# SwiGLU feed-forward on one core: the first 256 tokens of x in two loads instead of one, and the order of the first weight loads

## The chip, the core and the metric

The kernel runs on one core of one Trainium2 chip. The metric is the device time of one execution in microseconds (us), lower is better. The kernel before was run three times: 119.38, 119.57 and 120.18 us, median 119.57. One more execution was profiled; the profile and the trace come from that one.

A core has five engines that run side by side and meet at semaphores: TensorE (PE in the profile; its weight loads are PEld), VectorE (DVE), ScalarE (ACT), GpSimd (POOL) and SyncE (SP). SyncE and ScalarE each issue loads and stores through a DMA queue of their own (SPq and ACTq in the profile).

## The reference

```python
B, S, D, F = 1, 2048, 512, 1376      # all inputs bf16

def reference(x, w_gate, w_up, w_down):
    g = silu(x @ w_gate)             # [S, F]
    u = x @ w_up                     # [S, F]
    return (g * u) @ w_down          # [S, D]
```

## The kernel before, in words

**Tiles.** The 2048 tokens are worked on in four chunks of 512 (`SC`). The 512 inputs (`D`) are four contraction steps of 128 (`dk`). The 1376 hidden columns (`F`) are ten full tiles of 128 (`ft`) and a rest of 96. For each chunk and tile TensorE computes a gate group (`G`) and an up group (`U`) transposed: the weights are stationary, x is moving, and the result has hidden columns on partitions and tokens along the row. Each group has one PSUM bank and consists, for each `dk`, of two matmuls, one for each half of 64 columns (`tile_position=(0, m)`), which run side by side in two column halves of the array (`gu_step`, L353). ScalarE takes the silu of the gate group, VectorE multiplies it by the up group into `hT_sb`. The rests of the four chunks are packed into X groups (L417) and Y groups (L428). When all chunks are through, TensorE runs the down projection from `hT_sb` and `wd_sb` (L464, in strips of 32 rows, and L441, L516), and VectorE and ScalarE copy the results to `o_sb`, from where they are stored. TensorE works its list of groups from front to back; the order is written out by hand.

**The head, where the change lies.** x must lie with its inputs on partitions (`xT_sb`). Chunks 1 to 3 come so by transposing loads. For chunk 0 a transposing load would be late, so its first 256 tokens (`HT`) are loaded as they are into `xn_sb`, and TensorE transposes them with an identity matrix (`ident`, from an iota by GpSimd and a comparison by VectorE).

- TensorE first runs `N_WARM` = 6 matmuls of 512 columns on constants (L367), then `N_FILL` = 2 pairs of 128 columns on two halves of 64 rows (L372).
- It waits for `xn` and for `ident`. Token 2p + j lies on partition p, place j, so that a partition gets one contiguous piece of 2 KB. For `dk` = 0, 1, 2 it transposes in halves of 64 rows, four per `dk` (L382, 12 in all, the two halves into two banks), for `dk` = 3 in halves of 64 columns (L390, 4 in all).
- VectorE copies the results of `dk` 0 and 2 from PSUM to `xT_sb`, ScalarE those of 1 and 3 (four copies of 128 x 256). The group list calls them T groups.
- The first four groups, `g0, u0, g1, u1` (tiles 0 and 1), run first over the 256 tokens that were transposed: both gates interleaved by `dk`, then both ups. Then they run over the other 256 tokens: `g0` in two pieces of 128 (waiting for `x0b`, then for `x0c`), the others in one of 256. From tile 2 on, each matmul has all 512 tokens.

**The queues.** ScalarE issues one load at the start, the first slab of gate weights (`wg0`, tiles 0 and 1, 256 KB). SyncE issues, in this order: `xn` (256 KB), `wu0` (256 KB), the transposing loads `x0b` and `x0c` (128 tokens each), and then the gate and up slabs of tiles 2 to 10, x of chunks 1 to 3, the down weights and the stores. A wait on a load (`need`) is put in front of the first matmul that uses it; all that stands behind it on TensorE waits too.

The stores of token tiles 0 and 1 go through `rows_of`, which undoes the 2p + j order: each writes every second row of the first 256.

Of the kernel before, what the change touches and what calls it, by code (L numbers as in the profile page):

```python
# [6 lines left out]
BF16 = mybir.dt.bfloat16  # L7
FP32 = mybir.dt.float32

N_WARM = 6  # L10
N_FILL = 2


def bass_standalone__swiglu_ffn__prompt_kernel(nc, x, w_gate, w_up, w_down, out):
    _, S, D = x.shape
    F = w_gate.shape[1]
    P = 128
    KD = D // P
# [3 lines left out]
    SC = 512  # L22
# [7 lines left out]
    HT = SC // 2  # L30
    HC = P // 2
    NXN = HT // P
    NB = 8
    NSG = 4
    NOS = 8
    assert D == 512 and S % SC == 0 and KD == 4 and F_LAST == 96 and NSC % 2 == 0

    xf = x[0]
    of = out[0]


    UPH = F + 32
# [4 lines left out]
    with ExitStack() as es:  # L47
# [4 lines left out]
        xT_sb = sb("xT_sb", [P, KD, S], BF16)  # L52
# [23 lines left out]
        s_P = sem("s_P")  # L76
# [4 lines left out]
        rest = list(range(4 * NOS))  # L81

        def take(i):
            rest.remove(i)
            return s_dma[i]

        s_out = [take(i) for i in (8, 1, 2, 3, 4, 5, 7, 6)]
        homes = dict(xn=14, x0b=22, wg0=30, x0c=13, wu0=21, wg2=29, wu2=20, wg4=12, wu4=28, wg6=19)
        loads = {}

        def load_sem(name):
            loads[name] = take(homes[name] if name in homes else rest[0])
            return loads[name]

        ones_w = nc.const_aps.tensor(1.0, [P, P], BF16)
        ones_m = nc.const_aps.tensor(1.0, [P, SC], BF16)
# [3 lines left out]
        def load_x(eng, name, t0, t1):  # L100
            eng.dma_start_transpose(
                xT_sb[:, :, t0:t1], xf[t0:t1, :]
            ).then_inc(load_sem(name), 16)

        def load_w(eng, name, src, base, f0, f1):
            eng.dma_start(
                w_sb[:, :, base + f0:base + f1],
                src[:, f0:f1].rearrange("(k p) f -> p k f", p=P),
            ).then_inc(load_sem(name), 16)

        slabs = [(0, 2), (2, 4), (4, 6), (6, 8), (8, NFT)]
        slab_of = {ft: a for a, b in slabs for ft in range(a, b)}

        def load_slab(eng, a, b):
            load_w(eng, f"wg{a}", w_gate, 0, a * P, min(b * P, F))
            load_w(eng, f"wu{a}", w_up, UPH, a * P, min(b * P, F - 32))

        def loads_on_scalar(act):
            load_w(act, "wg0", w_gate, 0, 0, slabs[0][1] * P)

        def loads_on_sync(sp):
            sp.dma_start(
                xn_sb[:, :, :].rearrange("p j d -> p (j d)"), xf[0:HT, :].rearrange("(p j) d -> p (j d)", j=NXN)
            ).then_inc(load_sem("xn"), 16)
            load_w(sp, "wu0", w_up, UPH, 0, slabs[0][1] * P)
            load_x(sp, "x0b", HT, HT + P)
            load_x(sp, "x0c", HT + P, SC)
            for a, b in slabs[1:]:
                load_slab(sp, a, b)
            load_w(sp, "wut", w_up, F - (F - 32), F - 32, F)  # L130
            for c in range(1, NSC):
                load_x(sp, f"x{c}", c * SC, (c + 1) * SC)
            sp.dma_start(
                wd_sb[:, 0:NFF, :], w_down[0:NFF * P, :].rearrange("(k p) d -> p k d", p=P)
            ).then_inc(load_sem("wd"), 16)
            for c in range(NSC):
# [7 lines left out]
        groups = []  # L144
# [1 line left out]
        act_ops, dve_ops = [], []  # L146

        def add_group(kind, **what):
            g = dict(kind=kind, at=len(groups), bank=banks[turn[(len(groups) - KD) % NB]], readers=[], **what)
            groups.append(g)  # L150
            return g

        def add_op(eng, g, **what):
            n_read[eng] += 1
            op = dict(g=g, at=n_read[eng], **what)
            (act_ops if eng == "A" else dve_ops).append(op)
            if g:
                g["readers"].append((eng, op["at"]))
            return op

        def tview(dk):
            return psum[:, 2 * dk:2 * dk + 2, 0:HC].bitcast(BF16).rearrange("p h (i t) -> p h i t", i=NXN)

        def tview_last():
            return psum[:, 6, 0:P].bitcast(BF16).rearrange("p (i t) -> p i t", i=NXN)

        sg_reader = []
        n_sg = 0
# [55 lines left out]
                t_ready[c] = d["at"]  # L224

        xt_ready = {}
        for dk in range(KD):
            g = add_group("T", dk=dk)
            eng = "DA"[dk % 2]
            out = xT_sb[:, dk, 0:HT]  # L230
            if dk < KD - 1:
                out, src = out.rearrange("p (i h t) -> p h i t", i=NXN, h=2), tview(dk)
            else:
                out, src = out.rearrange("p (i t) -> p i t", i=NXN), tview_last()
            op = add_op(eng, g, kind="copy", out=out, src=src, stored=(None, 0))
            xt_ready[dk] = (eng, op["at"])
        NT = len(groups)

        for c in range(NSC):
            for fts in [[0], [1], [2, 3]] + [[ft] for ft in range(4, NFF)]:  # L240
# [8 lines left out]
        for at in range(NST):  # L249
            j, c = divmod(at, NSC)  # L250
            t = c * TPC + j
            ob = at % NOS
            end = at == NST - 1
            for c0, c1 in [(0, LASTA), (LASTA, LASTB), (LASTB, D)] if end else [(0, D)]:
                g = add_group("O", t=t, c0=c0, c1=c1, c=c)
                (quads[j] if c0 == 0 else last).append(g)
                eng = "A" if (end and c0 == 0) or (j < TPC - 1 and c % 2) else "D"
# [6 lines left out]
            n_store[ob] += 2 if end else 1  # L264

        def rows_of(t):
            if t < NXN:
                return of[0:HT, :].rearrange("(p j) d -> j p d", j=NXN)[t]
            return of[t * P:(t + 1) * P, :]

        def on_sync(sp):
# [48 lines left out]
        def on_tensor(pe):  # L320
            landed = set()

            def need(name):
                if name not in landed:
                    pe.wait_ge(loads[name], 16)
                    landed.add(name)
# [13 lines left out]
            def gu_step(g, dk, n0, n1):  # L340
                c, ft = g["c"], g["ft"]
                if c > 0:
                    need(f"x{c}")
                if c == 0 and n1 > HT:
                    need("x0b")
                if c == 0 and n1 > HT + P:
                    need("x0c")
                need(("wg" if g["kind"] == "G" else "wu") + str(slab_of[ft]))
                if c == 0 and n0 < HT:
                    after(*xt_ready[dk])  # L350
                col = (0 if g["kind"] == "G" else UPH) + ft * P
                for m in (0, HC):
                    ins = pe.matmul(  # L353
                        g["bank"][m:m + HC, n0:n1], lhsT=w_sb[:, dk, col + m:col + m + HC],
                        rhs=xT_sb[:, dk, c * SC + n0:c * SC + n1], start=(dk == 0), stop=(dk == KD - 1),
                        tile_position=(0, m),
                    )
                if n1 == SC and dk == KD - 1:
                    ins.then_inc(s_P, 1)

            def gu_matmuls(g, n0, n1):
                for dk in range(KD):
                    gu_step(g, dk, n0, n1)
# [4 lines left out]

            warm(N_WARM, SC)
            for i in range(N_FILL):  # L370
                for h in range(2):
                    pe.matmul(  # L372
                        banks[NB - 2 + h][:, 0:P], lhsT=ones_w[h * HC:(h + 1) * HC, :],
                        rhs=ones_m[h * HC:(h + 1) * HC, 0:P], start=True, stop=True, tile_position=(h * HC, 0),
                    )
            need("xn")
            pe.wait_ge(s_J, 1)
            for dk in range(KD - 1):
                for i in range(NXN):
                    for h in range(2):  # L380
                        t0 = h * HC
                        ins = pe.transpose(  # L382
                            tview(dk)[:, h, i, :], xn_sb[t0:t0 + HC, i, dk * P:(dk + 1) * P],
                            ident[t0:t0 + HC, t0:t0 + HC],
                        )
                ins.then_inc(s_P, 1)
            for i in range(NXN):
                for m in (0, HC):
                    c0 = (KD - 1) * P + m
                    ins = pe.transpose(tview_last()[m:m + HC, i, :], xn_sb[:, i, c0:c0 + HC], ident[:, :])  # L390
            ins.then_inc(s_P, 1)

            g0, u0, g1, u1 = groups[NT:NT + 4]
            for dk in range(KD):
# [1 line left out]
                    gu_step(g, dk, 0, HT)  # L396
            for g in (u0, u1):
                gu_matmuls(g, 0, HT)
            gu_matmuls(g0, HT, HT + P)
            gu_matmuls(g0, HT + P, SC)  # L400
            for g in (u0, g1, u1):
                gu_matmuls(g, HT, SC)

            for g in groups[NT + 4:]:
# [149 lines left out]
```

## Time and profile before

| | before |
|---|---|
| runs | 119.38, 119.57, 120.18 us (median 119.57) |
| profiled execution | 120.14 us, span of the instructions 118.8 us |
| PE busy | 116.1 us (98%) |
| DVE, ACT busy | 43.4 us (37%), 35.5 us (30%) |
| first warm-up matmul, first transpose, first gate matmul | start at 0.77, 3.61, 4.40 us |
| DMA | 8.92 MB, mean 75 GB/s over the span |

Times in the trace count from the start of the span. The page gives each engine's busy time and the chain of work that ended last; the timeline gives starts and lengths; the DMA view gives what a transfer took from its issue to its landing, which is when the waiting engine may go on. A matmul's duration contains its way through the array and overlaps with the next one's, so rates are read from starts or counts, not from sums of durations. The granted clock in the profile is 1.00 for the whole span; half speed at the start shows only in the durations of matmuls.

### The profile page before, as it was taken

The page shows a single profiled execution, that of the slowest core. Times are in us where ns is not written, and L with a number is a line of the kernel's source. Part 1 is how long each engine was busy: PE and PEld are TensorE (multiplying, and loading weights), DVE is VectorE, ACT ScalarE, POOL GpSimd, SP SyncE. Part 2 cuts the span into 40 slices and gives each one's busy share as a digit, 9 for nine tenths or more (in the row PEclk, how much of TensorE's full clock was granted, in tenths as well). Part 3 has the DMA queues.
Part 4 walks back from the last instruction along what each step waited for, and adds up shares of the span by engine and source line. Part 5 has one row for each costly group of instructions (what it writes and reads, how often), then busy time and mean ns, then how long its engine had stood idle before and what let it go on. Part 6 is the DMA issues. An engine that isn't in the chain of part 4 may idle for free.

```text
span 118.8 us, 2992 instructions
## 1 busy us (share of the span) xinstructions
PE 116.1 (98%) x1343; PEld 65.9 (55%) x1344; DVE 43.4 (37%) x68; ACT 35.5 (30%) x61; POOL 0.4 (0%) x5
## 2 busy tenths in 40 slices
PE   7999999999999999999999999999999999999993
PEld 2795555555555555555555555554444444464452
DVE  0123533442524442534452444369800040214331
ACT  5234234264243274242355232470000030213001
POOL 1000000000000000000000000000000000000000
DMA  2999999992000000000000000000000022023612
GB/s 90 271 280 341 204 218 189 296 312 49 0 6 0 0 0 6 0 0 6 0 6 0 0 0 0 6 0 0 6 0 6 0 88 95 0 90 106 207 44 88
DMA packets 17596, 8.92 MB, mean 75 GB/s; under 512 B 8624, under 2 KB 17456, under 8 KB 17584
## 3 DMA queue, kind: packets, MB, share of 16 engines
q1 hardware_dynamic: 16912, 8.38, 27.9%
q10 hardware_dynamic: 672, 0.36, 1.0%
q8 instruction: 10, 0.16, 0.6%
q14 instruction: 2, 0.02, 0.0%
HBM read 4.81 MB, written 2.10 MB: 58 GB/s over the span
## 4 chain that ended last, share of the span: by engine, by line
PE 98%; issue 0%; DVE 0%
PE psum L353 59%; PE psum L464 24%; PE psum L441 7%; PE psum L417 3%; PE psum L367 2%; PE psum L428 1%; PE psum L390 0%; PE psum L372 0%; PE psum L382 0%; DVE o_sb L317 0%; PE psum L516 0%
## 5 line engine op out<-in xcount | busy, mean ns | idle before, releaser
L353 PE MATMUL psum<-xT_sb,w_sb 128*64 128x512 bf16 (+2 forms) x680 | 70.5, 369 | 0.0
L353 PEld LDWEIGHTS psum<-xT_sb,w_sb 128*64 128x64 bf16 x680 | 42.6, 111 | 27.1
L313 DVE TENSOR_TENSOR hT_sb<-sg_sb,psum 128x512 bf16<-128x512 f32 x40 | 27.5, 688 | 41.0 <-PE psum L353 36.6
L299 ACT ACTIVATE sg_sb<-psum 128x512 f32<-128x512 f32 x40 | 23.8, 596 | 41.2 <-PE psum L353 41.1
L464 PE MATMUL psum<-wd_sb,hT_sb 32*128 32x512 bf16 x480 | 26.9, 374 | 0.0
L464 PEld LDWEIGHTS psum<-wd_sb,hT_sb 32*128 32x128 bf16 x480 | 12.9, 93 | 13.1 <-issue 0.4
L317 DVE CAST o_sb<-psum 128x512 bf16<-128x512 f32 (+1 forms) x11 | 6.4, 603 | 25.2 <-PE psum L464 19.9
L299 ACT ACTIVATE o_sb<-psum 128x512 bf16<-128x512 f32 (+1 forms) x7 | 3.7, 580 | 32.9 <-PE psum L464 25.9
L441 PE MATMUL psum<-wd_sb,hT_sb 128*128 128x512 bf16 (+2 forms) x59 | 8.7, 307 | 0.2 <-issue 0.2
L441 PEld LDWEIGHTS psum<-wd_sb,hT_sb 128*128 128x128 bf16 x60 | 4.6, 98 | 4.6 <-issue 0.4
L313 DVE TENSOR_TENSOR ht_sb<-sgy_sb,yu_sb 32x512 bf16<-32x512 f32 x8 | 5.5, 683 | 0.4
L417 PE MATMUL psum<-xT_sb,w_sb 128*64 128x512 bf16 x32 | 4.2, 379 | 0.0
L313 DVE TENSOR_TENSOR ht_sb<-sgx_sb,psum 32x512 bf16<-32x512 f32 x4 | 2.8, 692 | 3.5 <-ACT sgx_sb L299 3.5
L299 ACT ACTIVATE sgx_sb<-psum 32x512 f32<-32x512 f32 x4 | 2.4, 588 | 4.5 <-PE psum L417 4.5
L367 PE MATMUL psum<-const-bfloat16-1.0 128*128 128x512 bf16 x6 | 2.7, 623 | 0.8 <-PEq L539 0.8
L464 PE MATMUL psum<-wdt_sb,ht_sb 32*128 32x512 bf16 (+1 forms) x48 | 3.3, 371 | 0.0
L417 PEld LDWEIGHTS psum<-xT_sb,w_sb 128*64 128x64 bf16 x32 | 2.0, 110 | 1.4
L299 ACT ACTIVATE sgy_sb<-psum 64x512 f32<-64x512 f32 x4 | 2.4, 590 | 0.1
L464 PEld LDWEIGHTS psum<-wdt_sb,ht_sb 32*128 32x128 bf16 x48 | 1.3, 93 | 1.3
L428 PE MATMUL psum<-xT_sb,w_sb 128*64 128x512 bf16 x16 | 1.9, 379 | 0.0
L367 PEld LDWEIGHTS psum<-const-bfloat16-1.0 128*128 128x128 bf16 x6 | 0.7, 133 | 1.9 <-issue 1.9
L288 ACT ACT_TABLE_LOAD x1 | 1.3, 1283 | 1.2 <-PEq L539 1.2
(21 smaller groups left out, 7.7 us busy)
## 6 DMA issues: line engine op xcount, KB each, us to landing
out_dram<-o_sb SPq DMA_DIRECT2D x15, 128.0 KB, 1.8
wd_sb<-in_w_down_dram SPq DMA_DIRECT2D x1, 1280.0 KB, 8.8
w_sb<-in_w_up_dram SPq DMA_DIRECT2D x4, 256.0 KB, 4.2
w_sb<-in_w_gate_dram SPq DMA_DIRECT2D x3, 256.0 KB, 4.2
wdt_sb<-in_w_down_dram SPq DMA_DIRECT2D x4, 96.0 KB, 7.1
w_sb<-in_w_gate_dram SPq DMA_DIRECT2D x1, 352.0 KB, 6.1
w_sb<-in_w_up_dram SPq DMA_DIRECT2D x1, 320.0 KB, 5.7
w_sb<-in_w_gate_dram ACTq DMA_DIRECT2D x1, 256.0 KB, 3.6
```

Of the source, the lines that this page charges most:

```text
L288: act.activation(adummy[:, 0:4], zero_c, ACT.Silu)
L299: act.activation(op["out"], op["src"], fn).then_inc(s_A, 1)
L313: ins = dve.tensor_tensor(op["out"], op["a"], op["b"], ALU.mult)
L317: ins = dve.tensor_copy(op["out"], op["src"])
L353: ins = pe.matmul(g["bank"][m:m + HC, n0:n1], lhsT=w_sb[:, dk, col + m:col + m + HC], rhs=xT_sb[:, dk, c * SC + n0:c * SC + n1], start=(dk ...
L367: pe.matmul(banks[NB - 1][:, 0:width], lhsT=ones_w, rhs=ones_m[:, 0:width], start=True, stop=True)
L417: ins = pe.matmul(g["bank"][m:m + HC, :], lhsT=w_sb[:, dk, XC0 + m:XC0 + m + HC], rhs=xT_sb[:, dk, c * SC:(c + 1) * SC], start=(dk == 0), ...
L428: ins = pe.matmul(g["bank"][y0:y1, :], lhsT=w_sb[:, dk, YC0:YC0 + 64], rhs=xT_sb[:, dk, c * SC:(c + 1) * SC], start=(dk == 0), stop=(dk == ...
L441: ins = pe.matmul(g["bank"][:, 0:c1 - c0], lhsT=hT_sb[:, fk, t * P:(t + 1) * P], rhs=wd_sb[:, fk, c0:c1], start=(start and fk == 0), stop= ...
L464: ins = pe.matmul(g["bank"][:, 0:c1 - c0], lhsT=h(r, g["t"]), rhs=w[R * r:R * (r + 1), c0:c1], start=(start and n == 0), stop=final, tile_ ...
```

## The change

The 256 tokens are loaded in two halves of 128 (128 KB each): `xn0` by SyncE and `xn1` by ScalarE, each as the first request on its queue. Token j * 128 + p lies on partition p, place j, so a partition gets a piece of 1 KB from each load, and the 2p + j order is gone, in `rows_of` too. `wg0` moves from ScalarE's queue to SyncE's, behind `xn0`; `wu0` follows, and then one transposing load of 256 tokens (`x0b`) instead of two of 128.

All 16 transposes are done in column halves (64 columns of x stationary, 128 columns of the identity moving), two per T group, one T group for each half j and each `dk`. They run in the order of `t_order`, each group in a bank of its own, with the wait on `xn1` before the third group. There are eight copies of 128 x 128 instead of four of 128 x 256. Warm-up matmuls go from 6 to 4, fill pairs from 2 to 3, and these too are column halves. `g0`'s second half is one piece of 256 instead of two of 128.

The table of semaphores (`homes`, `load_sem`) is renamed to match; which semaphore a load gets has no part in the order.

```diff
-N_WARM = 6
-N_FILL = 2
+N_WARM = 4
+N_FILL = 3
...
+        def load_rows(eng, j):
+            eng.dma_start(xn_sb[:, j, :], xf[j * P:(j + 1) * P, :]).then_inc(load_sem(f"xn{j}"), 16)
+
         def loads_on_scalar(act):
-            load_w(act, "wg0", w_gate, 0, 0, slabs[0][1] * P)
+            load_rows(act, 1)
 
         def loads_on_sync(sp):
-            sp.dma_start(
-                xn_sb[:, :, :].rearrange("p j d -> p (j d)"), xf[0:HT, :].rearrange("(p j) d -> p (j d)", j=NXN)
-            ).then_inc(load_sem("xn"), 16)
-            load_w(sp, "wu0", w_up, UPH, 0, slabs[0][1] * P)
-            load_x(sp, "x0b", HT, HT + P)
-            load_x(sp, "x0c", HT + P, SC)
+            load_rows(sp, 0)
+            load_slab(sp, *slabs[0])
+            load_x(sp, "x0b", HT, SC)
             for a, b in slabs[1:]:
                 load_slab(sp, a, b)
...
+        t_bank = [[0, 4, 5, 6], [1, 2, 3, 7]]
+        t_order = [(0, 0), (0, 1), (1, 0), (0, 2), (1, 1), (0, 3), (1, 2), (1, 3)]
+
+        def tview(j, dk):
+            return psum[:, t_bank[j][dk], 0:HC].bitcast(BF16)
...
-        for dk in range(KD):
-            g = add_group("T", dk=dk)
+        for j, dk in t_order:
+            g = add_group("T", j=j, dk=dk)
             eng = "DA"[dk % 2]
...
+            op = add_op(
+                eng, g, kind="copy", out=xT_sb[:, dk, j * P:(j + 1) * P], src=tview(j, dk), stored=(None, 0),
+            )
             xt_ready[dk] = (eng, op["at"])
...
         def rows_of(t):
-            if t < NXN:
-                return of[0:HT, :].rearrange("(p j) d -> j p d", j=NXN)[t]
             return of[t * P:(t + 1) * P, :]
...
             for i in range(N_FILL):
-                for h in range(2):
+                for m in (0, HC):
                     pe.matmul(
-                        banks[NB - 2 + h][:, 0:P], lhsT=ones_w[h * HC:(h + 1) * HC, :],
-                        rhs=ones_m[h * HC:(h + 1) * HC, 0:P], start=True, stop=True, tile_position=(h * HC, 0),
+                        banks[NB - 1][m:m + HC, 0:P], lhsT=ones_w[:, m:m + HC], rhs=ones_m[:, 0:P],
+                        start=True, stop=True, tile_position=(0, m),
                     )
-            need("xn")
+            need("xn0")
             pe.wait_ge(s_J, 1)
-            for dk in range(KD - 1):
-                for i in range(NXN):
-                    for h in range(2):
...
+            for j, dk in t_order:
+                need(f"xn{j}")
+                for m in (0, HC):
+                    c0 = dk * P + m
+                    ins = pe.transpose(tview(j, dk)[m:m + HC, :], xn_sb[:, j, c0:c0 + HC], ident[:, :])
                 ins.then_inc(s_P, 1)
...
-            gu_matmuls(g0, HT, HT + P)
-            gu_matmuls(g0, HT + P, SC)
-            for g in (u0, g1, u1):
+            for g in (g0, u0, g1, u1):
                 gu_matmuls(g, HT, SC)
```

More of the change, by code (lines that the diff above doesn't have):

```diff
@@ L35, in bass_standalone__swiglu_ffn__prompt_kernel @@
     NOS = 8
+    NT = NXN * KD
     assert D == 512 and S % SC == 0 and KD == 4 and F_LAST == 96 and NSC % 2 == 0
@@ L87, in bass_standalone__swiglu_ffn__prompt_kernel @@
         s_out = [take(i) for i in (8, 1, 2, 3, 4, 5, 7, 6)]
-        homes = dict(xn=14, x0b=22, wg0=30, x0c=13, wu0=21, wg2=29, wu2=20, wg4=12, wu4=28, wg6=19)
+        homes = dict(xn0=14, xn1=22, wg0=30, x0b=13, wu0=21, wg2=29, wu2=20, wg4=12, wu4=28, wg6=19)
         loads = {}
         def load_sem(name):
-            loads[name] = take(homes[name] if name in homes else rest[0])
+            loads[name] = take(homes[name] if name in homes else next(i for i in rest if i not in homes.values()))
             return loads[name]
@@ L148, in add_group @@
         def add_group(kind, **what):
-            g = dict(kind=kind, at=len(groups), bank=banks[turn[(len(groups) - KD) % NB]], readers=[], **what)
+            g = dict(kind=kind, at=len(groups), bank=banks[turn[(len(groups) - NT) % NB]], readers=[], **what)
             groups.append(g)
@@ L159, in add_op @@
             return op
[L161 to L165, printed above, removed]
+        t_bank = [[0, 4, 5, 6], [1, 2, 3, 7]]
+        t_order = [(0, 0), (0, 1), (1, 0), (0, 2), (1, 1), (0, 3), (1, 2), (1, 3)]
+        def tview(j, dk):
+            return psum[:, t_bank[j][dk], 0:HC].bitcast(BF16)
         sg_reader = []
@@ L226, in bass_standalone__swiglu_ffn__prompt_kernel @@
         xt_ready = {}
-        for dk in range(KD):
-            g = add_group("T", dk=dk)
+        for j, dk in t_order:
+            g = add_group("T", j=j, dk=dk)
             eng = "DA"[dk % 2]
[L230 to L235, printed above, removed]
+            op = add_op(
+                eng, g, kind="copy", out=xT_sb[:, dk, j * P:(j + 1) * P], src=tview(j, dk), stored=(None, 0),
+            )
             xt_ready[dk] = (eng, op["at"])
-        NT = len(groups)
         for c in range(NSC):
@@ L345, in gu_step @@
                     need("x0b")
-                if c == 0 and n1 > HT + P:
-                    need("x0c")
                 need(("wg" if g["kind"] == "G" else "wu") + str(slab_of[ft]))
@@ L370, in on_tensor @@
             for i in range(N_FILL):
-                for h in range(2):
+                for m in (0, HC):
                     pe.matmul(
-                        banks[NB - 2 + h][:, 0:P], lhsT=ones_w[h * HC:(h + 1) * HC, :],
-                        rhs=ones_m[h * HC:(h + 1) * HC, 0:P], start=True, stop=True, tile_position=(h * HC, 0),
+                        banks[NB - 1][m:m + HC, 0:P], lhsT=ones_w[:, m:m + HC], rhs=ones_m[:, 0:P],
+                        start=True, stop=True, tile_position=(0, m),
                     )
-            need("xn")
+            need("xn0")
             pe.wait_ge(s_J, 1)
-            for dk in range(KD - 1):
-                for i in range(NXN):
-                    for h in range(2):
[L381 to L385, printed above, removed]
-                ins.then_inc(s_P, 1)
[L387 to L391, printed above, removed]
+            for j, dk in t_order:
[3 more added lines that the diff above has]
+                    ins = pe.transpose(tview(j, dk)[m:m + HC, :], xn_sb[:, j, c0:c0 + HC], ident[:, :])
+                ins.then_inc(s_P, 1)
             g0, u0, g1, u1 = groups[NT:NT + 4]
```

## The prediction

> **What bounds the kernel now.** I read the page first, then the chain of waits, then the first 5 us of the timeline, then the DMA view of that stretch. The page:
>
> ```profile
> PE 116.1 (98%) x1343; PEld 65.9 (55%) x1344; DVE 43.4 (37%) x68; ACT 35.5 (30%) x61; POOL 0.4 (0%) x5
> ...
> PE 98%; issue 0%; DVE 0%
> ```
>
> The chain that ends last is TensorE from beginning to end. In order of time (start, length, line, count) it begins:
>
> ```profile
> 0.77 2.72 PE psum L367 x6
> 3.49 0.33 PE psum L372 x4
> 3.82 0.32 PE psum L382 x12
> 4.14 0.36 PE psum L390 x4
> 4.50 18.08 PE psum L353 x200
> 22.57 0.86 PE psum L417 x8
> 23.43 17.27 PE psum L353 x160
> ```
>
> Two of these pieces do the same work. The 200 matmuls of the first L353 piece are 128 of 512 columns, 56 of 256 and 16 of 128: together 128 + 28 + 4 = 160 full ones, as in the second piece. That one takes 17.27 us, 0.108 us each. The first takes 18.08, or 18.17 from its first start at 4.40. So the projections of the first chunk lose 0.8 to 0.9 us, and I asked whether to a late transfer or to a slow clock. Matmuls by shape in 4.4 to 5.4 us, then in 6.0 to 6.7 us (count | busy, mean ns of one):
>
> ```profile
> L353 PE MATMUL psum<-xT_sb,w_sb 128*64 128x256 bf16 x10 | 1.3, 418 | 0.0
> ```
>
> ```profile
> L353 PE MATMUL psum<-xT_sb,w_sb 128*64 128x256 bf16 x18 | 1.2, 280 | 0.0
> ```
>
> The same instruction takes 418 ns early and 280 ns later, and twice as many pass per us: TensorE runs at half speed until 5.66 us, where the single records change. That is 1.26 us of gates at half speed, a loss of 0.63; narrow matmuls cost about 0.1 more. No transfer holds TensorE up once the gates run. So the change can act in three places only: when the gates start, when the clock turns to full speed, and whether a new hole opens. From 5.66 us to the end the work is fixed.
>
> What sets the start at 4.40 (start, length):
>
> ```profile
> 0.74 0.46 ACTq L106 DMA_DIRECT2D w_sb<-in_w_gate_dram  x1
> 0.74 0.41 SPq L122 DMA_DIRECT2D xn_sb<-in_x_dram  x1
> ...
> 1.21 0.41 SPq L106 DMA_DIRECT2D w_sb<-in_w_up_dram  x1
> ...
> 1.67 2.57 SPq L101 DMA_TRANSPOSE xT_sb<-in_x_dram  x2
> ...
> 4.28 0.58 SPq L106 DMA_DIRECT2D w_sb<-in_w_gate_dram  x1
> ```
>
> ```profile
> GB/s 0 0 0 0 0 0 0 0 0 0 0 0 0 0 147 197 147 262 180 311 328 201 115 319 324 316 348 352 336 340 356 344 344 340 334 320 309 295 226 213
> ...
> w_sb<-in_w_gate_dram ACTq DMA_DIRECT2D x1, 256.0 KB, 3.6
> xn_sb<-in_x_dram SPq DMA_DIRECT2D x1, 256.0 KB, 2.8
> ```
>
> The x load lands 2.8 us after 0.74, at 3.56; the first transpose starts at 3.61. The first gate weights land 3.6 after 0.74, at 4.30; the last of 16 transposes starts at 4.18, and the first gate at 4.40. Transposes and weights arrive together, so moving one alone gains nothing. The GB/s row has slots of 0.125 us: the first byte moves at 1.75 us, the first 1.1 us are slow (about 210 GB/s), then some 340.
>
> **The change, part by part.** (1) Warm-up: two matmuls go, starts 0.427 us apart, so 0.85 us; two fill pairs of 128 columns become three, 128/512 of 0.427 = 0.107 each. The first fill was at 3.42, so now 2.57, and the last ends at about 2.89. This was waiting time; its cover is the x load. Without that cover (x before 2.9) it would be a gain.
>
> (2) x: 128 KB on each queue instead of 256 KB on one. The nine slots from 1.75 to 2.875 add up to 1888, times 0.125 is 236 KB; 26 KB more are there at 2.96. A 128 KB store late in this trace lands 0.35 us after its last byte. If nothing comes between, all of x lands at 3.3; at the latest like the load of before, 3.56, as these are the same bytes in the same slow stretch. I take 3.45, between, and for the first half 3.1. The wait on the second half is new: behind it on TensorE stand six transpose pairs and all gates, and ScalarE and VectorE wait for these with six of their eight copies. ScalarE's table load follows its request at 1.23 as before.
>
> *Beside it:* the Trainium skill, "DMA: Bandwidth & Descriptors", section "Issuing engines are not separate DMA queues", says that two issuing engines share the same DMA engines and only issue time is saved. By that rule the second queue brings nothing and x lands at 3.56. The trace agrees so far: the ACT queue's first byte moves at 2.6 us, when SyncE's x is nearly through, though both were issued at 0.74.
>
> (3) Transposes: 8 pairs of 128 columns at 0.107 = 0.86 us, against 0.68 before (3.60 to 4.28). Two pairs need only the first half of x; six follow the second: 0.64. With 0.05 from landing to start and 0.12 to the first gate (4.28 to 4.40), transposes let the gates start 0.81 after x: at 4.26 (4.11 to 4.37).
>
> (4) Copies: eight of 128 columns for four of 256. Rows: 292 ns on VectorE and 384 on ScalarE for 256 columns; so 146 to 292 and 192 to 384. ScalarE has three after the second half of x; the first starts some 0.6 after it (three transpose pairs and their latency), so at 384 the last ends at 1.75. The fourth gate step wants it at 0.81 + 3 x 0.43 = 2.1 at half speed: hidden under the gates. At full speed it would be wanted at 1.46, and 0.3 lost.
>
> (5) Gate weights move from ScalarE at 0.74 to SyncE at 1.21, behind the first half of x. By bytes, x and these weights (524 KB) are through the GB/s row at 3.75, so they land at 4.1 at best. By rows of single loads they land 3.2 us after issue (the next gate slab, issued at 4.28) to 3.8 (the ups of before, issued at 1.21): 4.4 to 5.05. I take 4.3: SyncE's own ups no longer mix into them. Gates then start at 4.35, 0.05 earlier; at half speed that is worth 0.03.
>
> (6) Ups move from 1.21 to 1.67. By bytes (786 KB) they are through at 4.5 and land at 4.9; with the 3.8 of before, at 5.5. Needed at 5.8: slack 0.3 at least.
>
> (7) One transposing load of 256 tokens issues at 2.13. Two of 128 took 2.6 us of SyncE; the last of 512 took 2.2 (min/median/max of that line are 1.26/2.20/4.25), so it is over at 3.7 to 4.7. It lands at 5.9 by bytes, or 1.9 after the end of its issue as the second of before did: 5.6 to 6.6. Both halves of the first four groups come first: needed at 6.75. No stall; if the clock turned early, at 6.1, up to 0.5. SyncE reaches the next slab at 3.74 to 4.7 instead of 4.28. That slab landed at 7.44 and was used at 8.5, so 0.4 us later is covered, and the ups, later slabs and x chunks behind it have more (the next chunk of x lands at 17.5, used from 22.6).
>
> (8) Stores of tiles 0 and 1 write packed rows instead of every second row; both are 1 KB pieces, lie under 20 us of the down projection, and cost nothing.
>
> **Sum.** 0.03 gained, 0 to 0.1 lost in new small waits: nothing. The profiled execution took 120.14 us (span 118.8 and 1.36 around it), 0.57 over the median of 119.57. Its half-speed gates lost 0.63, so I put that difference to the clock's turn, which seems to move between runs (119.38 to 120.18). On the median: 119.6, by itself 119.2 to 120.0.
>
> **Rivals.** *The clock turns later* (the one on the slow side). TensorE was nearly gapless from 0.77 to 5.66, 4.9 us, before it ran at full speed. Now it idles after the fills (2.89 to 3.15), after two transpose pairs (3.36 to 3.5), and around 4.3: with the drain ahead of the fills some 0.6 us without work, and 0.86 of transposes beside it. If the turn hangs on how densely TensorE worked, holes postpone it. Each us of delay costs 0.5. If the count begins anew with the gates at 4.35, the turn comes at 4.35 + 4.9 = 9.25, 3.6 later: +1.8. If it only shifts by the holes: +0.3. It decides against the kernel (over 1%) from a turn 2.4 us later. Against it: before, too, had a 0.13 us drain and 0.68 of transposes in that stretch, and the clock turned. Price near the upper end, since the last hole lies right before the gates and one may be enough: 1.4, or 121.0.
>
> *Beside it:* the Trainium skill, "TensorE: Matmul & The Clock Gate", Part 1, says that the gate opens after a busy window of about 3.4 us, and that windows run freely. One window lost would be 3.4 / 2 = 1.7 us by its figure, an estimate: 121.3. The trace's 4.9 us from first matmul to full speed lies between one window and two.
>
> *x and weights land early.* With no 512 KB of other requests in front, two requests of 128 rows may fill all DMA engines sooner: x at 3.1, weights at 3.9, gates at 3.95. Gain 0.45 at half speed, 0.2 to 0.3 us: 119.3. For it speaks that the slow first 1.1 us holds half empty slots (115, 147); against it that every first load here begins so.
>
> *SyncE's queue is the bound.* Its order is strict, so the weights land at 4.8 to 5.05 and the gates start at 5.1: 0.7 late, 0.35 at half speed, and the transposing load may add up to 0.5: 119.9 to 120.5. For it: both loads behind the first on SyncE needed 3.8 to 4.0 us. Against: they waited for ScalarE's weights, which are gone.
>
> **How the numbers follow.** Forecast 0.38, clock later 0.37, early 0.10, SyncE's queue 0.15. About 1% (1.2 us) is what a measurement of this kernel can tell from no change. Slower by more: nearly all of the clock's 0.37 (0.35) and some of the queue's (0.04). Faster by more would need the gates at full speed 1.2 us sooner, before x can land: 0.05, for an early clock with early loads. Range 119.0 to 121.3.
>
> **What would show it.** Right: first gate at 4.2 to 4.4, 256-column matmuls at about 420 ns until 5 to 6 us, no hole after. Wrong: 420 ns rows beyond 8 us (the clock), a first gate after 4.7 (the queue), before 4.0 (early loads), or a hole at the second half of the first gate (the transposing load).

## The result, and the profile after

| | before | changed |
|---|---|---|
| median | 119.92 us (22 executions, 119.38 to 120.57) | 120.57 us (22 executions, 120.00 to 121.99) |
| ratio, 95% interval | | 1.0049, 1.0026 to 1.0072 |
| profiled execution | 120.14 us, span 118.8 | 121.82 us, span 120.5 |

The change makes the kernel slower by about 0.6 us, half a per cent. A ratio leaves out executions more than 1.5% above the fastest of their kernel; here these are four of the six that took 121.3 to 122.0 us, and the first profile is of one of them, so a second profile of the same kernel (120.48 us) stands beside it below.

The page of the changed kernel, and the head of its chain of waits:

```profile
PE 117.3 (97%) x1336; PEld 67.2 (56%) x1336; DVE 43.7 (36%) x70; ACT 35.6 (30%) x63; POOL 0.4 (0%) x5
...
PE 95%; DMA 2%; DVE 0%; issue 0%
```

```profile
0.74 2.90 DMA xn_sb<-in_x_dram
3.65 0.04 issue
3.69 1.06 PE psum L375 x13
4.75 19.52 PE psum L346 x192
24.27 0.86 PE psum L400 x8
25.14 17.27 PE psum L346 x160
```

The chain no longer begins with warm-up matmuls but with the load of x: TensorE waited for it. The projections of the first chunk (192 matmuls, again worth 160 full ones) take 19.52 us where 17.27 would do. The later chunks take what they took. The head of the timeline:

```profile
0.74 0.39 ACTq L120 DMA_DIRECT2D xn_sb<-in_x_dram  x1
0.74 0.40 SPq L120 DMA_DIRECT2D xn_sb<-in_x_dram  x1
...
1.20 0.44 SPq L107 DMA_DIRECT2D w_sb<-in_w_gate_dram  x1
...
2.57 0.53 PE L365 MATMUL psum<-const-bfloat16-1.0 128*64 128x128 bf16 x6
3.58 0.57 SPq L107 DMA_DIRECT2D w_sb<-in_w_gate_dram  x1
...
3.69 1.06 PE L375 MATMUL psum<-ident,xn_sb 128*64 128x128 bf16 x16 [0.59 <-DMA xn_sb<-in_x_dram]
```

The last fill starts at 2.78 and has streamed by 2.89; the first transpose starts at 3.69: 0.8 us with nothing to stream (the 0.59 shown counts from the modelled end of the last fill). The 16 transposes follow without a gap, 0.107 us a pair, and the first gate starts at 4.63 instead of 4.40. The DMA view of 0 to 5 us says why x was late:

```profile
GB/s 0 0 0 0 0 0 0 0 0 0 0 0 0 0 90 82 213 229 57 229 344 373 316 316 348 340 340 352 324 307 307 315 283 295 283 275 256 283 287 227
...
xn_sb<-in_x_dram ACTq DMA_DIRECT2D x1, 128.0 KB, 2.7
xn_sb<-in_x_dram SPq DMA_DIRECT2D x1, 128.0 KB, 2.9
```

Both halves land together, at 3.47 and 3.65, where the one load had landed at 3.56, and the first 1.1 us are as slow as they were (0.125 us a slot).

The 256-column matmuls of this execution at 8.0 to 8.7 us, then those of the second profile at 6.3 to 7.0:

```profile
L346 PE MATMUL psum<-xT_sb,w_sb 128*64 128x256 bf16 x12 | 1.5, 421 | 0.0
```

```profile
L346 PE MATMUL psum<-xT_sb,w_sb 128*64 128x256 bf16 x16 | 1.3, 309 | 0.0
```

In the first profile TensorE is still at half speed at 8.7 us, in the second it has just left it. I read the turn off the single records, where the gate and up matmuls become shorter than the 421 ns of half speed (the very first gate, with nothing ahead of it, is always shorter, some 390 ns): 8.87 and 6.19, against 5.66 before.

**One relation holds all profiles together.** Gates at half speed lose half their time, and the rest is fixed, so the span should be a constant plus (first gate + turn) / 2. With 113.8 us, and with the first gate in place of the turn where the clock had turned before it:

| profile | x landed (the later half) | ups landed | last of chunk 0's x | first gate | turn | by the relation | span |
|---|---|---|---|---|---|---|---|
| before | 3.56 | 5.05 | 6.13 | 4.40 | 5.66 | 118.8 | 118.8 |
| changed | 3.65 | 5.58 | 6.67 | 4.63 | 8.87 | 120.6 | 120.5 |
| a0_after (changed, again) | 3.65 | 5.72 | 6.81 | 4.48 | 6.19 | 119.1 | 119.1 |
| a1_warm6 | 3.68 | 5.99 | 7.03 | 4.58 | 5.87 | 119.0 | 119.0 |
| b1_warm4 | 3.60 | 5.12 | 6.18 | 4.42 | 9.30 | 120.7 | 120.6 |
| b2_loads | 3.50 | 5.80 | 6.90 | 4.41 | 5.87 | 118.9 | 118.9 |
| b3_transposes | 3.60 | 5.10 | 6.16 | 4.58 | 5.20 | 118.7 | 118.7 |
| b4_trans_warm4 | 3.65 | 5.14 | 6.23 | 4.63 | 8.80 | 120.5 | 120.4 |
| c1_x_on_sync | 4.38 | 5.15 | 6.19 | 5.16 | 7.69 | 120.2 | 120.2 |
| c2_fill10 | 3.68 | 5.81 | 6.85 | 4.58 | before 4.58 | 118.4 | 118.9 |
| e1_wg0_act | 3.61 | 5.15 | 6.19 | 4.56 | 5.63 | 118.9 | 118.9 |
| e2_x0_two | 3.55 | 5.91 | 7.00 | 4.71 | before 3.7 | 118.5 | 118.8 |
| f1_mended | 3.63 | 4.91 | 6.23 | 5.21 | 6.49 | 119.7 | 119.6 |
| g1_old_transposes | 3.33 | 5.50 | 6.56 | 4.75 | 9.44 | 120.9 | 120.8 |

In these two profiles all gates run at full speed. In c2_fill10 the last transposes (4.38 us) still have the half-speed spacing of 0.107 us. In e2_x0_two the transposes are fast already: twelve in halves of 64 rows take 0.35 us, against 0.53 before. The gates of c2_fill10 from 4.55 to 5.4 us, then the transposes of e2_x0_two:

```profile
L346 PE MATMUL psum<-xT_sb,w_sb 128*64 128x256 bf16 x16 | 1.1, 274 | 0.0
```

```profile
3.64 0.35 PE L382 MATMUL psum<-ident,xn_sb 64*128 64x64 bf16 x12
```

Only there, with the gate weights on SyncE and the clock early, is the span longer than the relation, by 0.5 and 0.3 us: TensorE waits for loads behind the gates, as shown below.

### The profile page after: what moved, and what is told of

Its sections match the earlier page's. It is cut to its first block, busy times and chain, and to the rows that moved or that the text cites. A ratio compares the mean times of both kernels' runs of the same rounds, so it can differ in the third digit from the quotient of the medians.

```text
span 120.5 us, 2981 instructions
## 1 busy us (share of the span) xinstructions
PE 117.3 (97%) x1336; PEld 67.2 (56%) x1336; DVE 43.7 (36%) x70; ACT 35.6 (30%) x63; POOL 0.4 (0%) x5
## 4 chain that ended last, share of the span: by engine, by line
PE 95%; DMA 2%; DVE 0%; issue 0%
PE psum L346 59%; PE psum L447 24%; PE psum L424 7%; PE psum L400 3%; DMA xn_sb<-in_x_dram 2%; PE psum L411 1%; PE psum L375 1%; DVE o_sb L312 0%; PE psum L499 0%
## 5 line engine op out<-in xcount | busy, mean ns | idle before, releaser
L346 PE MATMUL psum<-xT_sb,w_sb 128*64 128x512 bf16 (+1 forms) x672 | 72.0, 378 | 0.0
L346 PEld LDWEIGHTS psum<-xT_sb,w_sb 128*64 128x64 bf16 x672 | 44.0, 114 | 27.1
L447 PE MATMUL psum<-wd_sb,hT_sb 32*128 32x512 bf16 x480 | 26.9, 374 | 0.0
L447 PEld LDWEIGHTS psum<-wd_sb,hT_sb 32*128 32x128 bf16 x480 | 12.7, 93 | 13.2 <-issue 0.4
L447 PE MATMUL psum<-wdt_sb,ht_sb 32*128 32x512 bf16 (+1 forms) x48 | 3.3, 371 | 0.0
L400 PEld LDWEIGHTS psum<-xT_sb,w_sb 128*64 128x64 bf16 x32 | 2.0, 110 | 1.4
L360 PE MATMUL psum<-const-bfloat16-1.0 128*128 128x512 bf16 x4 | 1.9, 619 | 0.8 <-PEq L522 0.8
L447 PEld LDWEIGHTS psum<-wdt_sb,ht_sb 32*128 32x128 bf16 x48 | 1.3, 93 | 1.3
L312 DVE COPY xT_sb<-psum 128x128 bf16<-128x128 bf16 x4 | 0.8, 223 | 2.8 <-PE psum L375 2.7
L375 PE MATMUL psum<-ident,xn_sb 128*64 128x128 bf16 x16 | 1.1, 314 | 0.6 <-DMA xn_sb<-in_x_dram 0.6
```

The costliest lines, as they stand in the source:

```text
L312: ins = dve.tensor_copy(op["out"], op["src"])
L346: ins = pe.matmul(g["bank"][m:m + HC, n0:n1], lhsT=w_sb[:, dk, col + m:col + m + HC], rhs=xT_sb[:, dk, c * SC + n0:c * SC + n1], start=(dk ...
L360: pe.matmul(banks[NB - 1][:, 0:width], lhsT=ones_w, rhs=ones_m[:, 0:width], start=True, stop=True)
L375: ins = pe.transpose(tview(j, dk)[m:m + HC, :], xn_sb[:, j, c0:c0 + HC], ident[:, :])
L400: ins = pe.matmul(g["bank"][m:m + HC, :], lhsT=w_sb[:, dk, XC0 + m:XC0 + m + HC], rhs=xT_sb[:, dk, c * SC:(c + 1) * SC], start=(dk == 0), ...
L447: ins = pe.matmul(g["bank"][:, 0:c1 - c0], lhsT=h(r, g["t"]), rhs=w[R * r:R * (r + 1), c0:c1], start=(start and n == 0), stop=final, tile_ ...
```

## The experiments

All times are compared with the kernel before, run on the same chip in the same rounds.

**The short warm-up (a0_after, a1_warm6, b1_warm4).** The changed kernel again; the changed kernel with the old warm-up; the kernel before with the short warm-up alone.

```diff
 # a1_warm6, from the changed kernel
-N_WARM = 4
-N_FILL = 3
+N_WARM = 6
+N_FILL = 2
 # b1_warm4, from the kernel before
-N_WARM = 6
-N_FILL = 2
+N_WARM = 4
+N_FILL = 3
```

> The changed kernel again, unaltered, for the spread of its executions and a second profile. Theory A (the clock: TensorE stands idle from the end of the fills at 2.9 us to x at 3.7 us, and this hole postpones the turn to full speed): ratio about 1.005, some executions more than 1 us above the others; in the profile the 256-column matmuls change from 421 to 273 ns later than the 5.7 us of before, at 6 to 9 us. Theory B (the start: x lands 0.1 us later and the transposes take 0.95 instead of 0.8 us, so the gates start 0.23 us later, and the clock turns where it likes): ratio about 1.002, gates at 4.6 us, the turn anywhere between 4 and 6 us as in the kernel before.

> The changed kernel with the old warm-up: six matmuls of 512 columns and two fill pairs, so that TensorE has work until 3.65 us, when x lands. Theory A: the hole is closed, the late executions go, ratio 1.001 to 1.002 (what is left are the later gates). Theory B: the gates still start at 4.6 us, so nothing changes against the changed kernel, ratio 1.005.

> The kernel before with the new number of warm-up matmuls alone (four, and three fill pairs in its own halves of 64 rows). TensorE then idles from 2.9 to 3.6 us. Theory A: slower, ratio 1.003 to 1.005, with some executions 1.5 us above the others, and a turn to full speed after 6 us more often. Theory B: the gates start at 4.4 us as before, ratio 1.000.

Measured: a0_after 1.0077 (1.0047 to 1.0107; 12 executions, 120.01 to 122.11), a1_warm6 1.0041 (1.0020 to 1.0063; none above 120.86), b1_warm4 1.0134 (1.0095 to 1.0174; 6 executions, 120.97 to 121.99). The chain of b1_warm4:

```profile
3.60 0.05 issue
3.65 0.50 PE psum L382 x9
4.15 0.36 PE psum L390 x4
4.50 19.86 PE psum L353 x200
```

Its gates start as before (4.42), all its loads land as before, and yet the 200 matmuls take 19.86 us instead of 18.08: nothing has changed but the warm-up, with a hole ahead of the transposes where two matmuls were, and the turn comes at 9.30. By the relation (and 1.35 us around the span) all six executions turned between 7.2 and 9.3 us. So theory A holds, with a price well above its 1.003 to 1.005: the shorter warm-up postpones the turn. Whether the idle time does it or the smaller amount of work is not told apart by closing the hole, since that adds work too; c1_x_on_sync below, with one matmul less than before but a hole of 0.9 us among its transposes, turned at 7.69 and speaks for the idle time. But a1_warm6 did not come back to 1.001 to 1.002, and the changed kernel, with the same hole, turns late in only six executions of 22 (121.3 us and more) and five of 12 in a0_after (121.2 and more). Something else costs, and something else helps.

**The transposes (b3_transposes, b4_trans_warm4).** The kernel before with the new transposes and copies alone, then with the short warm-up as well.

```diff
 # both, from the kernel before
-for dk in range(KD - 1): ...        # 12 in halves of 64 rows, then 4 in halves of 64 columns
+for j, dk in t_order: ...           # 16 in halves of 64 columns
 # b4_trans_warm4 besides
-N_WARM = 6
-N_FILL = 2
+N_WARM = 4
+N_FILL = 3
```

> The kernel before with the new transposes and copies alone (16 in column halves, eight banks, eight copies); the loads, their order and the number of warm-up matmuls are the old ones, the fills are in column halves. Theory B: all eight transpose pairs now follow x, 0.86 us instead of 0.68, so the gates start 0.1 to 0.2 us later, ratio 1.001 to 1.002. Theory A: no hole, so nothing beyond that.

> The old loads with the new transposes and the short warm-up (four matmuls, three fill pairs in column halves). Idle from 2.9 to 3.65 us, as in the kernel with the short warm-up alone, which turned at 9.3 us and cost 1.3%. Theory A1 (the hole alone decides, whatever transposes follow it): late turns in nearly all executions, ratio 1.012 to 1.015. Theory A2 (the hole is half made good by the column transposes, which keep all of TensorE busy for 0.75 us where the old ones use it in small pieces): a mixture as in the changed kernel, most executions turning at 5 to 7 us, ratio 1.005 to 1.008.

Measured: b3_transposes 1.0030 (1.0005 to 1.0056), b4_trans_warm4 1.0086 (1.0055 to 1.0117; 9 executions, 119.97 to 121.76). The gates start 0.18 us later (4.58): by the relation 0.09 us or 0.0008, at the lower edge of the interval; whether the turn moves too is not settled. With the short warm-up the same hole that sent all six executions of b1_warm4 past 120.9 leaves five of nine below it, a mixture as in the changed kernel. The ratio lies between the two forecasts, nearer to A2's: eight pairs in column halves right after the hole (and fills of that form ahead of it) make up for part of it. Transposes and fills changed together, so which of them does it is open. What exactly is counted, the traces don't show.

**The old transposes in the changed kernel (g1_old_transposes).** New loads and short warm-up, with transposes, copies and fills in halves of 64 rows as before.

```diff
 # from b2_loads, below
-N_WARM = 6
-N_FILL = 2
+N_WARM = 4
+N_FILL = 3
```

> The changed kernel with the transposes, copies and form of the fills of before: new loads and short warm-up (four matmuls, three fill pairs in halves of 64 rows). The last of the eight combinations of warm-up, loads and transposes. If the column transposes and fills are what keeps the changed kernel from the late turns of the short warm-up alone, nearly all executions turn late here: ratio 1.010 to 1.016, none below 120.7. If the new loads are what helps (x in two halves), a mixture as in the changed kernel: ratio 1.005 to 1.008, lowest near 120.2.

Measured: 1.0132 (1.0087 to 1.0178), six executions from 121.21 to 122.14. So it is the new transposes and fills, not the new loads, that keep the changed kernel from the late turns in most executions. Its profile has a second hole, though, which b1_warm4's has not: its gate weights landed at 4.70, and TensorE waited 0.47 us for them. The cleaner pair is b1_warm4 against b4_trans_warm4.

**The loads (b2_loads).** The kernel before with the new loads alone; its transposes wait for both halves.

```diff
-act: wg0            sp: xn, wu0, x0b, x0c
+act: xn1            sp: xn0, wg0, wu0, x0b (256 tokens)
```

> The kernel before with the new loads alone: x in two halves on two queues, gate weights, ups and one transposing load of 256 tokens on SyncE; warm-up, transposes and copies are the old ones (and wait for both halves). So far every profile fits span = 113.8 us + (first gate + turn to full speed) / 2. Theory A (the warm-up hole and the transposes make the difference, not the loads): the halves land at 3.5 and 3.65, transposes start 0.1 later than before, gates at 4.45 to 4.5, ratio 1.000 to 1.001. Theory C (the loads cost: the one transposing load lands at 6.7 to 7.0 instead of 6.1 and TensorE waits for it): ratio 1.002 or more and a hole ahead of the second half of the first gate.

Measured: 1.0067 (1.0035 to 1.0099), executions from 120.25 up. The time is theory C's. The gates start at 4.41, and the profile shows no hole, since its clock turned at 5.87. What shows is the lower end: before, executions go down to 119.43 in the same rounds, here none is below 120.25. The reason is seen in an execution whose clock turned early.

**Many short fills (c2_fill10).** Meant for the clock; it caught this wait too.

```diff
-N_FILL = 3
+N_FILL = 10
```

> The changed kernel with ten fill pairs instead of three, so that the four warm-up matmuls of 512 columns are followed by 1.07 us of pairs of 128 columns and TensorE has work until 3.64 us. Theory A (a hole is what postpones the clock, whatever closes it): no late executions, ratio as with six warm-up matmuls, 1.004. Rival (only the long matmuls count): late executions stay, ratio 1.006 to 1.008.

Measured: 1.0038 (1.0017 to 1.0060), 12 executions, none above 120.74. Short fills close the hole as well as long matmuls. In this profile the clock had turned before the first gate (4.58 us). Its chain between 3 and 9 us:

```profile
1.66 4.15 DMA w_sb<-in_w_up_dram
5.81 0.04 issue
5.85 3.19 PE psum L346 x49
```

At full speed the gates are through at 5.5 and TensorE waits nearly 0.4 us for the first ups, which land at 5.81, and after the last of them (6.64) once more for the transposing load (6.85). That gives each kernel a floor. The second half of the first gate starts 32 matmuls after the first gate, 1.75 us at full speed, and from there to the end it is 113.8 - 1.75 = 112.05 us of span and 1.35 around it. With chunk 0's x at 6.67 to 6.81 an execution of the changed kernel can't be below 120.1 to 120.2 (lowest measured 120.00), one of b2_loads with 6.90 not below 120.3 (120.25). The kernel before needs its last 128 tokens 0.22 us later and has them at 6.13. By the same sum that allows 119.3, while gates from 4.40 at full speed throughout allow 113.8 + 4.40 + 1.35 = 119.55 (lowest measured 119.38, without a profile): there this load holds nothing up. The floor moves with the landing of each execution: c2_fill10, with 6.85 in its profile, has one at 119.70.

**Whose fault is the late transposing load (e1_wg0_act, e2_x0_two)?** Both from b2_loads.

```diff
 # e1_wg0_act
-act: xn1            sp: xn0, wg0, wu0, x0b (256)
+act: xn1, wg0       sp: xn0, wu0, x0b (256)
 # e2_x0_two
-act: xn1            sp: xn0, wg0, wu0, x0b (256)
+act: xn1            sp: xn0, wg0, wu0, x0b (128), x0c (128); first gate's second half in two pieces
```

> The kernel before with the new loads alone, but the gate weights on ScalarE's queue, behind the second half of x; the one transposing load of 256 tokens stays. With the gate weights on SyncE the ups landed at 5.6 to 6.0 us and the transposing load at 6.7 to 7.0, against 5.05 and 6.15 before, and where the clock turned early TensorE waited for both. Theory D1 (the gate weights ahead of them on the same queue hold them up): ups at 5.1 to 5.2, transposing load at 6.2, no execution held at 120.25, lowest near 119.5, ratio 1.000 to 1.002. Theory D2 (the one large transposing load is what is late and drags the ups): still 5.8 and 6.9, lowest 120.2, ratio 1.006.

> The kernel before with the new loads alone, but two transposing loads of 128 tokens as before; the gate weights stay on SyncE. Theory D1: ups still at 5.6 to 6.0, the second transposing load at 6.7 to 7.0, lowest execution 120.2, ratio 1.005 to 1.007. Theory D2: ups at 5.1, transposing loads at 5.7 and 6.2, ratio 1.000 to 1.002.

Measured: e1_wg0_act 0.9999 (0.9975 to 1.0023; lowest 119.68), e2_x0_two 1.0013 (0.9989 to 1.0037; lowest 119.82). By the landings it is D1: in all seven profiles with the gate weights on SyncE the ups land at 5.5 to 6.0 and the last of x at 6.6 to 7.0, in all seven others at 4.9 to 5.15 and 6.1 to 6.25, in one load or in two. The DMA traffic of 4.0 to 6.4 us (0.06 us a slot), the changed kernel and then e1_wg0_act:

```profile
GB/s 290 265 299 290 290 307 252 286 235 269 265 303 265 303 265 260 158 166 107 94 60 43 34 137 179 290 294 277 290 299 286 305 320 316 290 252 282 239 282 77
```

```profile
GB/s 307 333 324 341 307 341 299 346 312 299 299 290 282 282 290 260 269 256 303 282 290 286 303 278 304 321 329 341 337 307 324 273 137 94 316 324 367 333 350 300
```

With the gate weights on SyncE, ahead of the ups and the transposing load, the engines run nearly dry at 5.0 to 5.4 us, in the middle of that load; e1_wg0_act has no such gap. The kernel before runs dry as well, but only behind its transposing loads, whose last packets start at 5.64:

```profile
GB/s 333 358 350 350 324 320 324 320 329 299 303 299 261 218 196 213 243 282 278 290 277 290 282 163 137 188 107 94 34 85 43 9 17 17 154 196 239 256 307 375
```

All 14 traces divide so: with the gate weights on SyncE the traffic first falls below 115 GB/s after 351 to 470 of the 1024 packets of the transposing loads (the only ones of 256 bytes here), otherwise after at least 1011 of them. Why it falls off is not shown. But in time two loads help as well (1.0013): 128 tokens land at 6.49, and the first gate goes on with them. So D2's time came true by another way than D2: the one load needs both its halves before anything starts. e1_wg0_act has a price of its own: two of its 12 executions took 122.1 and 122.3 us. Its gate weights now land at 4.52 instead of 4.25, and the gates start at 4.56.

**Both halves on SyncE (c1_x_on_sync).**

```diff
-act: xn1            sp: xn0, wg0, wu0, x0b       N_WARM = 4, N_FILL = 3
+act: wg0            sp: xn0, xn1, wu0, x0b       N_WARM = 5, N_FILL = 3
```

> The changed kernel with both halves of x on SyncE's queue, one behind the other, and the gate weights on ScalarE's as before; five warm-up matmuls, so that TensorE has work until 3.3 us. Asks whether the first half can land early at all. In the changed kernel the two queues shared the engines and both halves landed together (3.5 and 3.65). If the sharing was the reason: first half at 3.1 to 3.3, second at 3.55, gates at 4.4 to 4.45, hardly a hole, ratio 1.001. If the slow first microsecond of the DMA engines is the reason: both halves near 3.5, a hole of 0.2 to 0.3 us, gates at 4.5, ratio 1.003.

Measured: 1.0153 (1.0124 to 1.0182). Neither theory. The timeline:

```profile
3.31 0.42 PE L376 MATMUL psum<-ident,xn_sb 128*64 128x128 bf16 x4
...
4.43 0.85 PE L376 MATMUL psum<-ident,xn_sb 128*64 128x128 bf16 x12 [0.69 <-DMA xn_sb<-in_x_dram]
```

The first half lands at 3.14, early as hoped, but the second only at 4.38: ScalarE's gate weights, issued at 0.74, go between them and land at 4.02. So a second request on one queue can fall behind the first of the other, whatever is needed first.

**Both causes undone (f1_mended).** The changed kernel with six warm-up matmuls, two fill pairs, and the gate weights on ScalarE behind `xn1`.

> The changed kernel with both suspected causes undone: six warm-up matmuls and two fill pairs, and the gate weights on ScalarE's queue behind the second half of x. New transposes and the one transposing load stay. If warm-up, queue and transposes are all there is, what is left is the transposes' share (gates at 4.55 instead of 4.40): ratio 1.001 to 1.003, lowest near 119.6, none over 121. If something else costs, 1.004 as with the warm-up alone undone.

Measured: 1.0033 (1.0001 to 1.0065), 119.82 to 122.02. Lower than a1_warm6 at its best, but wide: two executions lie over 121, where none was expected. Its chain names the reason in the profiled execution:

```profile
1.18 3.99 DMA w_sb<-in_w_gate_dram
```

The gate weights landed at 5.17, after the ups (4.91), which are first on the other queue behind the first half of x, and the gates started at 5.21. In e1_wg0_act the same loads stand in the same order on the same queues, and there the gate weights landed first, at 4.52, and the ups at 5.15: which of the two queues is served first differs from profile to profile. No kernel tried here beats the kernel before; e1_wg0_act equals it.

**The parts together.** With the three parts of the change on and off:

| warm-up | loads | transposes | kernel | ratio (95%) |
|---|---|---|---|---|
| new | old | old | b1_warm4 | 1.0134 (1.0095 to 1.0174) |
| old | new | old | b2_loads | 1.0067 (1.0035 to 1.0099) |
| old | old | new | b3_transposes | 1.0030 (1.0005 to 1.0056) |
| new | new | old | g1_old_transposes | 1.0132 (1.0087 to 1.0178) |
| new | old | new | b4_trans_warm4 | 1.0086 (1.0055 to 1.0117) |
| old | new | new | a1_warm6 | 1.0041 (1.0020 to 1.0063) |
| new | new | new | changed | 1.0049 (1.0026 to 1.0072); a0_after 1.0077 (1.0047 to 1.0107) |

Each part alone makes the kernel slower, and they do not add up: the three alone would come to 2.3%. The reason lies in the relation. The floor that the loads set is felt only by executions that turn before about 6 us; what makes the turn late hides it. And the new transposes and fills, a cost alone, take back a good part of what the short warm-up costs. How much of the 0.5% belongs to which part, these intervals can't say. Nor is the warm-up the only thing that goes with late executions: of the five kernels with six warm-up matmuls and x in two loads, three (b2_loads, e1_wg0_act, f1_mended) had four executions of 34 at 121.9 to 122.3 us, where the kernel before had none above 120.61. No profile shows one of these.

## Why the prediction was right or wrong

The forecast was no change (119.6, 0.03 us gained and up to 0.1 lost). What came is half a per cent slower: within the 1% that was called no change, and outside the sum, 119.2 to 120.0 against 120.57. The sum stood on a median of three runs, 119.57; over 22 executions the kernel before takes 119.92. The size came out, the reasons only in part: the sum put at nothing the two costs that the runs show, the late turn of the clock and the late transposing load, and had no term for what the new transposes take back of the first. That it all stayed within 1% is luck.

- *Where it can act.* Right: first gate, turn and holes among the gates explain every span in the table.
- *(1) Warm-up.* The fills end at 2.89 as worked out, but "waiting time" was the wrong price. The hole costs through the clock: 1.3% alone on the kernel before, and late turns in 6 of 22 executions here.
- *(2) x.* The later half was taken at 3.45, at the latest 3.56, and lands at 3.65; the first was taken at 3.1 and lands with it. The two halves move side by side, from 1.8 and 2.0 us to 3.0 and 3.1, and the later one lands 0.54 us after its last packet starts, where the sum took 0.35 from a store. The sum by the rule of the Trainium skill ("DMA: Bandwidth & Descriptors", section "Issuing engines are not separate DMA queues") was nearer: the queues share the engines, and it gave 3.56.
- *(3) Transposes.* 0.107 us a pair is right; but as the halves land together, nearly all eight pairs follow x instead of six, and the gates start at 4.48 and 4.63, not 4.35. By half their delay this is 0.04 to 0.12 us.
- *(4) Copies.* 225 and 277 ns, hidden, as said.
- *(5) Gate weights.* Taken at 4.3; 4.21 and 4.35 in the changed kernel. Right, though two other kernels with that order had them at 4.66 and 4.70.
- *(6), (7) Ups and transposing load.* The steps that failed in size. Ups: at most 5.5 allowed, 5.58 and 5.72 measured. Transposing load: 5.6 to 6.6 allowed, 6.67 and 6.81 measured. The wait "if the clock turned early, up to 0.5" was named and then costed at nothing, because the sum was made for the one profiled execution, whose clock turned at 5.66. The executions that turn earlier are just those that make the kernel before fast. With the loads alone none is left below 120.25.
- *(8) Stores.* No trace of them in the difference: the later chunks and the down projection (28.60 us in L447) are unchanged.
- *Rivals.* "The clock turns later" foresaw a turn at 9.25 and +1.8 us at most; the profiled execution turned at 8.87 and stood 1.68 us above the profile of before. Right in mechanism and size, in 6 executions of 22, so it does not set the median. Of the signs of being wrong, the first profile shows the clock's (420 ns rows beyond 8 us); the second shows none of them. Its weak spot was what it counted against itself, that the transposes of before had not kept the clock from turning: with the short warm-up they did (b1_warm4), and the new ones mostly don't. "SyncE's queue" had the right place and the wrong load: late is what stands behind the gate weights. "x and weights land early" fell.

## What to carry to other kernels

A profile shows one execution. Where the executions of a kernel spread, ask what a transfer's slack is in the fastest of them: a wait that the profiled execution hides can be the floor of the others. And a warm-up that ends before the data comes is not free, though it only fills waiting time; here a hole of 0.75 us cost the kernel before 1.3%.

## What the runs showed of the hardware

- A shorter warm-up, with a hole of 0.75 us ahead of the transposes (2.9 to 3.65 us, b1_warm4), moved TensorE's turn to full speed from 6.5 us at the latest (by the relation, over the executions of before) to 7.2 to 9.3. The Trainium skill ("TensorE: Matmul & The Clock Gate", Part 1) tells of windows of 3.4 us; the profiled turns of b1_warm4 and before, 9.30 and 5.66, lie 3.6 apart, which is near one, but no run here shows a window itself.
- Without such a hole the turn is no fixed time after the first matmul (0.77 us): it came before 3.7 us in e2_x0_two, between 4.4 and 4.6 in c2_fill10, and at 5.2 to 6.5 in the other profiles.
- Eight transpose pairs in column halves, with fills of that form, make good part of such a hole (1.0086 against 1.0134); twelve transposes in halves of 64 rows and four in column halves don't.
- Two requests of 128 KB issued at the same moment on two queues landed within 0.21 us of each other in all nine profiles that have them. A second request on one queue landed behind the first of the other in c1_x_on_sync (3.14, 4.02, 4.38 us); of two second requests issued together, the gate weights landed first in one profile (e1_wg0_act) and the ups in another (f1_mended).
- With x, gate weights and ups (640 KB) ahead of the transposing load on one queue, the DMA engines fell to 34 to 107 GB/s for 0.3 us in the middle of that load (5.1 to 5.4 us, changed kernel). With 512 KB or less ahead of it on its queue they did not, and four requests in a row are not the reason, since c1_x_on_sync and the kernel before have them too. The cause stays open.
